# Twelve scatters ahead of a branch, and weight conversions on VectorE begun at the second step, in an attention, mixture-of-experts and MLP kernel

## The chip, the cores and the metric

The kernel runs on one core of one Trainium2 chip. The metric is the device time of one execution in microseconds (us). TensorE is PE in the profile, its weight loads are PEld, VectorE is DVE, ScalarE is ACT, GpSimd is POOL and SyncE, which issues most transfers, is SP.

## The reference

```
attn = attention of q, k, v (2 x 8 heads x 768 x 64), only between tokens whose 6 sign bits agree
x    = attn as 1536 rows of 512
logits = x @ w_gate + log1p(exp(x @ w_noise)) * noise          # 8 experts
top 2 experts of a row, their softmax as weights
out[row] += weight * (relu(x[row] @ w1[e]) @ w2[e])            # e = 0..7, 512 -> 1024 -> 512
h = out @ w_in;  g = h - tanh(h);  result = g @ w_out          # 512 -> 2048 -> 512, weights given as float64
```

## The kernel before

The program has three stages. Attention comes first, then the experts, then the last pair of products. Products are done in split form: an operand is a rounded high part and a low rest, and three matmuls make one product, so each weight tile is copied to `wt` by ScalarE (line 1004) and its low part is made by a subtraction on VectorE or GpSimd (line 1003).

The expert stage works through nine segments in a loop over `n`. Segments 0 and 1 are the two parts of expert 0, and segment `n` from 2 on is expert `n - 1`. A segment has eight steps `f`, one for each 128 columns of the hidden layer. A step does the first product of step `f + 1` (`both_step`, line 1269, and 1276 for a tail), lets ScalarE and VectorE move its result out of PSUM (lines 1300 and 1302), and then does the second product of step `f` (`y_step`, lines 1309 to 1311). Two PSUM banks take turns for the first product. After the last step `y_out` copies the four result banks out (lines 1334 to 1341), and the next segment's tail matmuls wait for the last of these copies.

Behind the products each step has a body, in this order: at its `f` a load of the next segment's rows (`load_x`, lines 1209 and 1212), weight fetches, `store`, transposes of the next segment's rows (`trans_x`, lines 1222 to 1224), conversion steps (`convert_more`), the fetch of the next 64-bit weights (`fetch64`), and one weight tile more (`next_w`). Everything on all five engines is issued in the order in which the program text has it (a manual schedule), so each engine works its instructions off in that order.

The rows of a segment are brought together by scattering. The late batch's gate (`gate(B - 1)`) finds each row's place among the experts' rows, `pick` turns it into indices `sidx`, and `scatter` sends twelve indirect DMAs of 128 rows from GpSimd to `Xg` in DRAM. Segment 1's rows come another way (`gather_x`, two indirect DMAs at line 832), the segments from 2 on are loaded from `Xg`. Between the place and the scatters the gate also makes the experts' counts (`totals`, `excess`), from which the engines take branches. One of them is `overflow`, an arm for rows that don't fit, which isn't taken here.

The last stage's weights arrive as 64-bit floats. `fetch64` loads 1 MB into one of two buffers `cv_t`, and `convert` turns it into float32 in six steps: line 1073 with ScalarE's 1071 in front of it, 1075, 1077, 1079, 1082 and the add at 1084. There are 16 such tiles, 96 steps. `convert_more(n)` takes `n` steps.

Of the kernel before, what the change touches and what calls it, by code (L numbers as in the profile page):

```python
# [6 lines left out]
F32 = mybir.dt.float32  # L7
# [8 lines left out]
ALU = mybir.AluOpType  # L16
# [33 lines left out]

POOL1 = 7

CV1 = 3

CVN = 2

KEEP = 8

ADD = (3, 4, 5, 6)

FA = 4

# [28 lines left out]
def body(tc, q, k, v, proj, w_gate, w_noise, noise, w1, w2, w_in, w_out, out):  # L91
    nc = tc.nc
    PS = bass.MemoryType.PSUM
    B, H, S, D = q.shape
# [22 lines left out]
    with ExitStack() as ctx:  # L117
# [66 lines left out]
        start = ExitStack()  # L184
# [106 lines left out]
        hd = {}  # L291
# [376 lines left out]
        def gate(b):  # L668
            w = lambda name, shape, dt=F32: gx.tile(shape, dt, name=name)
            early = b < B - 1  # L670
# [9 lines left out]
            u = w("g_u", [128, NC, E])  # L680
# [108 lines left out]
            if early:  # L789
# [2 lines left out]
                eng.tensor_scalar(capv[:, 1, 0:1], late0, -1.0, float(CAP), op0=ALU.mult, op1=ALU.add)  # L792
                eng.tensor_copy(basev[:, 1, 0:1], late0)
                eng.tensor_scalar(late0, late0, float(1 - FIRST), None, op0=ALU.add)
            yield
            if not early:
                yield from totals()
                yield from excess()
            ts = w("g_ts", [128, NC, E])
            if early:  # L800
                eng.tensor_scalar(ts, over, BIG, None, op0=ALU.mult)
# [3 lines left out]
            gd[b] = (oh, over, t, v8, e12)  # L805
            for _ in pick(sidx[:, :, b], oh, ts, eng, lead):
                yield

        def hot(b, c):

# [102 lines left out]
        def totals():  # L913
            tot = bank("a")
            for b in range(B):
                for c in range(NC):
                    nc.tensor.matmul(tot[:, b * E:(b + 1) * E], onesb, M[:, b, c], start=(b == 0 and c == 0),
                                     stop=(c == NC - 1), skip_group_check=True)
            for c in range(BC):
                nc.tensor.matmul(tot[:, B * E:(B + 1) * E], onesb, M[:, 1, c], start=False, stop=(c == BC - 1), skip_group_check=True)  # L920
            nc.vector.tensor_copy(tots, tot[:, 0:(B + 1) * E].rearrange("p (b e) -> p b e", b=B + 1))
            yield
            nc.vector.tensor_tensor(cnt, tots[0:1, 0], tots[0:1, 1], op=ALU.add)
            nc.vector.tensor_tensor(cnt[:, 0:1], cnt[:, 0:1], basev[0:1, 1, 0:1], op=ALU.add)
            pick_arms(0, 0, 1)

        def excess():
            nc.vector.tensor_tensor(exs, tots[:, 0], tots[:, 1], op=ALU.add)
            nc.vector.tensor_tensor(exs, exs, capv[:, 1], op=ALU.subtract)
            nc.vector.tensor_scalar(exs, exs, 0.0, None, op0=ALU.max)  # L930
            yield
            cmx = gx.tile([128, 1], F32, name="cmx")
            nc.vector.tensor_reduce(cmx, exs, op=ALU.max, axis=AX.X)
            nc.vector.tensor_copy(cmi, cmx)
            yield
            pick_arms(1, 1, E)
            yield
# [127 lines left out]
        def convert(f, t):  # L1065

            two = lambda dt: t.rearrange("p t n -> p (t n)").bitcast(dt).rearrange("p (n two) -> p n two", two=2)
            hi = two(I32)[:, :, 1]
            tl = lambda name, dt: hd["cvp"].tile([128, 2 * DM], dt, name=name)
            g, p, a, w = tl("cv_g", F32), tl("cv_p", I32), tl("cv_a", I32), tl("cv_w", F32)  # L1070
            nc.scalar.activation(g, two(F32)[:, :, 1], AF.Abs)

            nc.vector.tensor_scalar(g, g, _f32(896 << 20), None, op0=ALU.max)
            yield
            nc.vector.tensor_scalar(p, g.bitcast(I32), 3, 0x3FFFFFF8, op0=ALU.logical_shift_left, op1=ALU.bitwise_and)
            yield
            nc.vector.scalar_tensor_tensor(a, hi, _i32(0xC0000000), p, op0=ALU.bitwise_and, op1=ALU.bitwise_or)
            yield
            nc.vector.tensor_scalar(p, a, _i32(0xFF800000), None, op0=ALU.bitwise_and)
            yield  # L1080
            u = p.bitcast(F32)
            nc.vector.scalar_tensor_tensor(u, two(U32)[:, :, 0], 2.0 ** -52, u, op0=ALU.mult, op1=ALU.mult)  # L1082
            yield
            (nc.gpsimd if hd["n"] in ADD else nc.vector).tensor_tensor(w, u, a.bitcast(F32), op=ALU.add)  # L1084
            stores.append(lambda: nc.sync.dma_start(out=W2f[f], in_=w))
            yield

        def convert_more(n):

            for _ in range(n):  # L1090
                if hd.get("cv") is None and RAW64:
                    hd["cv"] = convert(*RAW64.pop(0))
                if hd.get("cv") is not None and next(hd["cv"], 1) is not None:
                    hd["cv"] = None
                    if RAW64:
                        hd["cv"] = convert(*RAW64.pop(0))
                        next(hd["cv"])
# [16 lines left out]
        def run(f, *a_):  # L1114
            for _ in f(*a_) or ():
                pass
# [118 lines left out]
        def load_arm(n):  # L1235
            e, b = segs[n][:2]
            AV[n] = nc.tensor.value_load(arm[0:1, e:e + 1], min_val=0, max_val=3)
# [225 lines left out]
            fn_()  # L1463
        fill(left[0], KEEP)
        load_arm(1)
        run(scatter, B - 1, 0)
        run(scatter, B - 1, 1)
        start.close()

        mid, late = ExitStack(), ExitStack()  # L1470

# [168 lines left out]
        def put_out():  # L1640
# [11 lines left out]
        manual = lambda: sched.enter_context(tc.manual_schedule(engines={nc.tensor.engine, nc.vector.engine, nc.scalar.engine,  # L1652
                                                                         nc.gpsimd.engine, nc.sync.engine}))
        overflow()
        manual()
        while fn[0] < wn[0] + 4:
            fetch()
# [18 lines left out]
        for n in range(1, NSG):  # L1676
            last = n == NSG - 1
            if last:
                store()
                mid.close()  # L1680
                del rings["st"]
                rings["C2"] = ctx.enter_context(tc.tile_pool(name="wC2", bufs=WC2, reuse_waits="tile"))
                rings["C"] = ctx.enter_context(tc.tile_pool(name="wC", bufs=WC, side="right", reuse_waits="tile"))
                rings["st"] = late.enter_context(tc.tile_pool(name="stC", bufs=2, side="right", reuse_waits="tile"))
            fx = 0 if n <= B else 1
            if n == B:
                free_gate()
            for f in seg_steps(n, (lambda: h2_step(at(0), None)) if last else (lambda: both_step(n + 1, 0))):
                if not last and f == fx:
                    load_x(n + 1)  # L1690
                if last and f == 4:
                    del rings["st"]
                    held_n = fn[0] - 1
                while fn[0] < min(wn[0] + (PF if "st" in rings or n < B else 2), len(wsrc)):
                    fetch()
                store()
                if not last and f == FA:
                    load_arm(n + 1)
                for dc in range(0 if last else KD4):
                    if f == (5 + dc // 2 if n == B - 1 else 3 + dc):  # L1700
                        trans_x(n + 1, dc)
                if n < B:
                    rests(2)
                    assert f < NF - 1 or not rest
                if n > B:
                    next(sort, None)
                if (B, CV1) <= (n, f) < (NSG - 1, 0):
                    hd["n"] = n
                    convert_more(CVN + (n in ADD and f % 4 == 1))
                if (B, 0) <= (n, f) < (NSG - 1, 0):  # L1710
                    while conv64 and len(RAW64) + (hd.get("cv") is not None) < (1 if (n, f) < (B, CV1) else 2):
                        fetch64(conv64.pop(0))
                for j in range(BC if last else 0):
                    if f == j:
                        gather(j)
                    if f == MIX[j]:
                        mix(j)
                        flush(1)
                for j in range(BC if last else 0):
                    if f == JOIN[j]:  # L1720
                        combine(j)
                        flush(1)
                if n >= B or f >= W1:
                    next_w()
                if B <= n < B + WN0 - NF and f == 4 or last and f in TWO:
                    next_w()
                if last and f == 6:
                    assert not [m for m in RAW if m <= held_n]
                    late.close()
                    m2 = ctx.enter_context(tc.tile_pool(name="m2", bufs=2, side="right", reuse_waits="tile"))  # L1730
                    gb2 = m2.tile([128, 1], F32, name="gb2")
                    nc.vector.memset(gb2, G2 / (2 * G3))
                    gsb = m2.tile([128, 1], F32, name="gsb")
                    nc.vector.memset(gsb, -GS)
# [7 lines left out]
        for n in range(-LA, len(steps2)):  # L1742
# [4 lines left out]
            blk, f = at(n + LA) or (NBK, 0)  # L1747
# [47 lines left out]
```

## Time and the profile before

| | |
|---|---|
| median of 3 runs | 888.33 us (886.56 to 890.89) |
| the profiled execution | 892.47 us |
| its span in the trace | 890.7 us |
| TensorE busy | 866.2 us, 97% of the span |
| VectorE, ScalarE, GpSimd busy | 655.6, 536.6, 437.0 us |

The span runs from the first to the last instruction that the profiler recorded. The profiled execution took 1.8 us more than its span, and 4.1 us more than the median of the runs without a profile. All instants below are microseconds from the start of the span.

### The profile page before, as it was taken

How to read it: one execution, taken by the hardware profiler on the slowest of the kernel's cores; microseconds unless marked ns; L12 is line 12 of the kernel's file. 1: busy time of each engine (PE TensorE's matmuls, PEld its weight loads, DVE VectorE, ACT ScalarE, POOL GpSimd, SP SyncE). 2: the span in 40 equal slices, each digit the busy share in tenths (PEclk: the TensorE clock that was granted, in tenths of full speed). 3: DMA queues.
4: the chain of work that ended last, by engine and by line, in shares of the span. 5: the costliest groups of instructions: out<-in, count | busy, mean ns of one | idle time of the engine just before them, and what ended most of it. 6: DMA issues, size and time to landing. Idle time of an engine off the chain costs nothing. (4 is left out here: it accounts for less than half of the span.)

```text
span 890.7 us, 13686 instructions
## 1 busy us (share of the span) xinstructions
PE 866.2 (97%) x4622; PEld 677.3 (76%) x4622; DVE 655.6 (74%) x1261; ACT 536.6 (60%) x1027; POOL 437.0 (49%) x403
## 2 busy tenths in 40 slices
PE   8999999999989979999999999999999999999998
PEld 3556555555546869898879898888889999999996
DVE  7688778778745644888697879867987677677665
ACT  6677668767435234544434445456787677677765
POOL 6787787798876354025312217720432632632322
PEclk9999999999989999999999999999999999999999
DMA  5546645511242467896799697784300200210000
GB/s 125 134 128 198 206 136 167 162 25 40 81 148 84 130 224 240 267 321 195 249 297 316 213 322 234 241 298 137 95 24 1 84 24 1 72 36 1 25 13 36
DMA packets 111980, 127.52 MB, mean 143 GB/s; under 512 B 33744, under 2 KB 82944, under 8 KB 111888
## 3 DMA queue, kind: packets, MB, share of 16 engines
q1 hardware_dynamic: 106880, 110.81, 39.6%
q0 software_dynamic: 5008, 15.49, 5.2%
q8 instruction: 57, 0.93, 0.4%
q14 instruction: 35, 0.29, 0.1%
HBM read 82.81 MB, written 41.18 MB: 139 GB/s over the span
## 5 line engine op out<-in xcount | busy, mean ns | idle before, releaser
L1309 PE MATMUL bank<-wt,hh 128*128 128x512 f32 (+1 forms) x392 | 156.2, 399 | 2.4 <-PEq L1247 1.2
L1588 POOL TENSOR_TENSOR g_th<-g_h,g_th 128x384 f32<-128x384 f32 x64 | 67.1, 1049 | 181.6 <-ACT g_th L1587 181.0
L1311 PE MATMUL bank<-wt,hh 128*128 128x512 f32 (+1 forms) x392 | 155.4, 396 | 0.4 <-DVE hh L1302 0.3
L1310 PE MATMUL bank<-wt,hh 128*128 128x512 f32 (+1 forms) x392 | 154.3, 394 | 0.0
L1269 PE MATMUL bank<-xh,wt 128*128 128x400 f32 (+3 forms) x512 | 140.2, 338 | 0.0
L443 DVE TENSOR_REDUCE mx<-bank 128x1 f32<-128x384 f32 x192 | 103.2, 551 | 42.9 <-PE bank L442 34.3
L478 ACT ACTIVATE p<-bank 128x384 f32<-128x384 f32 x192 | 91.9, 489 | 69.3 <-PE bank L477 56.9
L1269 PEld LDWEIGHTS bank<-xh,wt 128*128 128x128 f32 x512 | 93.7, 191 | 1.4
L1004 ACT ACTIVATE wt<-wraw 128x1024 fp32r<-128x1024 f32 x75 | 78.8, 1055 | 21.4 <-PE bank L1311 17.9
L1084 POOL TENSOR_TENSOR cv_w<-cv_p,cv_a 128x1024 f32<-128x1024 f32 x12 | 33.5, 2792 | 114.7 <-DVE cv_p L1082 46.3
L1311 PEld LDWEIGHTS bank<-wt,hh 128*128 128x128 f32 (+1 forms) x392 | 73.4, 187 | 19.4 <-DVE hh L1613 1.8
L1309 PEld LDWEIGHTS bank<-wt,hh 128*128 128x128 f32 (+1 forms) x392 | 73.8, 188 | 17.5 <-issue 2.7
L1231 PE MATMUL bank<-xh,wt 128*128 128x384 f32 x256 | 86.2, 337 | 0.0
L1229 PE MATMUL bank<-xh,wt 128*128 128x384 f32 x256 | 86.1, 336 | 0.0
L511 POOL TENSOR_TENSOR ps<-ps,p 128x768 f32<-128x768 f32 x45 | 82.4, 1830 | 7.4 <-ACT p L478 2.9
L1230 PE MATMUL bank<-xl,wt 128*128 128x384 f32 x256 | 85.9, 336 | 0.0
L1269 PE MATMUL bank<-xl,wt 128*128 128x400 f32 (+3 forms) x256 | 85.3, 333 | 0.3 <-DVE xl L1224 0.3
L502 PE MATMUL bank<-p,v 128*64 128x384 f32 x384 | 84.5, 519 | 0.9 <-issue 0.9
L1300 ACT ACTIVATE hh<-bank 128x448 fp32r<-128x448 f32 (+2 forms) x72 | 36.2, 503 | 79.0 <-issue 25.4
L1310 PEld LDWEIGHTS bank<-wt,hh 128*128 128x128 f32 (+1 forms) x392 | 73.6, 188 | 13.2
L476 PE MATMUL bank<-qc,kb 108*128 108x384 f32 (+1 forms) x192 | 79.3, 413 | 2.7 <-issue 1.6
L1003 DVE TENSOR_TENSOR wt<-wraw,wt 128x1024 fp32r<-128x1024 f32 (+1 forms) x64 | 75.3, 1182 | 5.2 <-ACT wt L1004 4.9
(318 smaller groups left out, 1864.2 us busy)
## 6 DMA issues: line engine op xcount, KB each, us to landing
wraw<-in_moe_w_dram SPq DMA_DIRECT2D x118, 256.0 KB
cv_t<-in_moe_w_in_dram SPq DMA_DIRECT2D x16, 512.0 KB
cv_t<-in_moe_w_out_dram SPq DMA_DIRECT2D x16, 512.0 KB
W2f<-cv_w SPq DMA_DIRECT2D x16, 512.0 KB
wraw<-W2f SPq DMA_DIRECT2D x16, 512.0 KB
Xg<-zero SPq DMA_DIRECT2D x14, 512.0 KB
xy<-Xg SPq DMA_DIRECT2D x7, 768.0 KB
Y<-xy SPq DMA_DIRECT2D x7, 768.0 KB
```

Of the source, the lines that this page charges most:

```text
L443: nc.vector.tensor_reduce(MX[i % 2][:, c, hf:hf + 1], ps[:, :HF], op=ALU.max, axis=AX.X)
L476: nc.tensor.matmul(ps[:, :HF], KB[sn(g, par)][r, ck(kc)], QC[sn(g, par)][r, half(hf)], start=True, stop=False)
L478: nc.scalar.activation(hd["p", i, kc][:, half(hf)], ps[:, :HF], AF.Exp, scale=float(D) ** -0.5)
L502: nc.tensor.matmul(hd["o", i][hf * D:(hf + 1) * D, :HF], raw["v", g][:, par, kc], hd["p", i, kc][:, half(hf)], start=(kc == 0), stop=(kc = ...
L511: eng.tensor_tensor(t, hd["p", i, 0] if kc == 1 else t, hd["p", i, kc], op=ALU.add)
L1229: nc.tensor.matmul(ps[:, :n], ws(0, dc), xh[:, dc, :n], start=(dc == 0), stop=False)
L1230: nc.tensor.matmul(ps[:, :n], ws(0, dc), xl[:, dc, :n], start=False, stop=False)
L1231: nc.tensor.matmul(ps[:, :n], ws(1, dc), xh[:, dc, :n], start=False, stop=(dc == KD4 - 1))
L1269: nc.tensor.matmul(col(ps), t[:, w_, 0, ck(dc)], col(x_[l_][:, dc]), start=(dc == 0 and (w_, l_) == (0, 0)), stop=(dc == KD4 - 1 and w_ == 1))
L1309: nc.tensor.matmul(ps[:m], a, t[:, 0, 1], start=first, stop=False)
L1310: nc.tensor.matmul(ps[:m], a, t[:, 1, 1], start=False, stop=False)
L1311: nc.tensor.matmul(ps[:m], l, t[:, 0, 1], start=False, stop=last)
```

## The change

Three things are changed in the program text. First, in the late batch's gate `pick` now comes directly behind the places, and `totals` and `excess` follow it; one `yield` of that gate is gone. Second, the manual schedule of the first stage is closed before the late batch's scatters, and a schedule of its own for GpSimd holds over them and over `overflow`, so that GpSimd's twelve scatters come in front of its branch in the order of the text. Third, all adds of the conversion are VectorE's (before, those of segments 3 to 6 were GpSimd's); the conversion begins at step 1 of segment 2 and not at step 3, which also moves the second `fetch64` two steps ahead; and the third conversion step in some steps stands in segment 2 at `f` = 1, 4 and 7, where before it stood in segments 3 to 6 at `f` = 1 and 5.

```diff
-CV1 = 3
+CV1 = 1
 CVN = 2
-ADD = (3, 4, 5, 6)
@@ gate
-            yield
-            if not early:
-                yield from totals()
-                yield from excess()
+            if early:
+                yield
             ts = w("g_ts", [128, NC, E])
@@ gate
             for _ in pick(sidx[:, :, b], oh, ts, eng, lead):
                 yield
+            if not early:
+                yield from totals()
+                yield from excess()
@@ convert
-            (nc.gpsimd if hd["n"] in ADD else nc.vector).tensor_tensor(w, u, a.bitcast(F32), op=ALU.add)
+            nc.vector.tensor_tensor(w, u, a.bitcast(F32), op=ALU.add)
@@ body
         load_arm(1)
+        start.close()
+        order_p = ExitStack()
+        order_p.enter_context(tc.manual_schedule(engines={nc.gpsimd.engine}))
         run(scatter, B - 1, 0)
         run(scatter, B - 1, 1)
-        start.close()
@@ body
         overflow()
+        order_p.close()
         manual()
@@ the loop over segments
                 if (B, CV1) <= (n, f) < (NSG - 1, 0):
-                    hd["n"] = n
-                    convert_more(CVN + (n in ADD and f % 4 == 1))
+                    convert_more(CVN + (n == B and f % 3 == 1))
                 if (B, 0) <= (n, f) < (NSG - 1, 0):
                     while conv64 and len(RAW64) + (hd.get("cv") is not None) < (1 if (n, f) < (B, CV1) else 2):
                         fetch64(conv64.pop(0))
```

## Rows read from the trace of the kernel before

**Rows 1.** Who TensorE waited for, whole span: us in total, times, longest.
```profile
PE bank L1222 <- DMA xy<-Xg: 6.3, 1, 6.3
PE bank L1276 <- DVE xy L1341: 2.4, 3, 2.0
...
PE bank L1276 <- DVE hh L1302: 0.6, 1, 0.6
```

**Rows 2.** TensorE's timeline: start, us, what [idle before it <- releaser].
```profile
332.69 1.98 PE L1222 MATMUL bank<-ident,xy 128*128 128x128 f32 x8 [6.26 <-DMA xy<-Xg]
...
357.42 0.40 PE L1309 MATMUL bank<-wt,hh 128*128 128x512 f32 x1
```

**Rows 3.** Stretches: engines' busy us (instructions), then the granted TensorE clock, DMA share, GB/s.
```profile
332.69:337.06 4.37, 4.37 (x21) 4.19 (x22) 1.25 (x2) 2.03 (x3) 0.78 (x1) 0.50 1.11 344
...
463.36:466.82 3.46, 3.46 (x8) 2.73 (x9) 3.43 (x6) 0.55 (x1) 0.00 (x0) 0.51 1.06 392
```

**Rows 4.** GpSimd's timeline, 297 to 327 us.
```profile
297.91 0.96 POOL L832 DMA_INDIRECT xy<-Xd,xidx  x1 [0.30 <-issue]
302.27 1.77 POOL L851 DMA_INDIRECT Xg<-x,sidx  x1 [3.40 <-DVE sidx L847]
...
314.40 0.98 POOL L851 DMA_INDIRECT Xg<-x,sidx  x1 [6.49 <-DMA Xg<-x,sidx]
...
325.29 0.98 POOL L851 DMA_INDIRECT Xg<-x,sidx  x1 [0.30 <-issue]
```

**Rows 5.** Instructions of the overflow branch: ns min/median/max, first and last start.
```profile
L1474 POOLq EVENT_SEMAPHORE  x4: 17/43/3947, 304.7 to 309.1; - x4
```

**Rows 6.** VectorE's timeline, 296 to 302 us.
```profile
296.33 0.20 DVE L788 TENSOR_TENSOR T<-bank,basev 128x48 f32<-128x48 f32 x1
...
301.01 0.19 DVE L804 SCALAR_TENSOR_TENSOR g_ts<-g_ov,T 128x48 f32<-128x48 f32 x1
...
301.81 0.17 DVE L847 CAST sidx<-g_p 128x12 int32<-128x12 f32 x1
```

**Rows 7.** Timeline of SyncE's queue, 328 to 358 us.
```profile
328.10 0.34 SPq L1209 DMA_DIRECT2D xy<-Xg  x1
...
349.61 0.53 SPq L1062 DMA_DIRECT2D cv_t<-in_moe_w_out_dram  x1
...
357.43 0.70 SPq L1062 DMA_DIRECT2D cv_t<-in_moe_w_out_dram  x1
```

**Rows 8.** Who SyncE's queue waited for, 345 to 361 us.
```profile
SPq L1062 <- DMA cv_t<-in_moe_w_out_dram: 0.3, 1, 0.3
```

**Rows 9.** ScalarE's timeline, 349 to 362 us.
```profile
349.42 0.54 ACT L1300 ACTIVATE hh<-bank 128x448 fp32r<-128x448 f32 x1 [2.91 <-issue]
349.86 1.05 ACT L1004 ACTIVATE wt<-wraw 128x1024 fp32r<-128x1024 f32 x1
...
360.58 1.14 ACT L1071 ACTIVATE cv_g<-cv_t 128x1024 f32<-128x1024 f32 x1
```

**Rows 10.** Timeline of VectorE, 361 to 364 us.
```profile
361.75 0.69 DVE L1073 TENSOR_SCALAR cv_g<-cv_g 128x1024 f32<-128x1024 f32 x1 [0.41 <-ACT cv_g L1071]
...
363.09 1.22 DVE L1003 TENSOR_TENSOR wt<-wraw,wt 128x1024 fp32r<-128x1024 f32 x1
```

**Rows 11.** Instructions on the tile `cv_p`: ns min/median/max, first and last start.
```profile
L1075 DVE TENSOR_SCALAR cv_p<-cv_g x16: 683/694/1672, 362.5 to 566.4; 128x1024 int32<-128x1024 int32 x16
L1077 DVE SCALAR_TENSOR_TENSOR cv_a<-cv_t,cv_p x16: 1206/1224/1716, 365.8 to 569.8; 128x1024 int32<-128x1024 int32 x16
...
L1084 POOL TENSOR_TENSOR cv_w<-cv_p,cv_a x12: 2393/2685/3328, 385.6 to 535.5; 128x1024 f32<-128x1024 f32 x12
L1084 DVE TENSOR_TENSOR cv_w<-cv_p,cv_a x4: 1225/2196/2207, 372.4 to 575.7; 128x1024 f32<-128x1024 f32 x4
```

**Rows 12.** Timelines of GpSimd and VectorE at 456 us.
```profile
455.94 2.40 POOL L1084 TENSOR_TENSOR cv_w<-cv_p,cv_a 128x1024 f32<-128x1024 f32 x1 [14.89 <-DMA W2f<-cv_w]
...
456.14 2.75 DVE L1073 TENSOR_SCALAR cv_g<-cv_g 128x1024 f32<-128x1024 f32 x1 [0.40 <-ACT cv_g L1071]
```

## The prediction, made before the result was known

> **What bounds the kernel now.** I read TensorE's waits first. TensorE works through almost the whole span, so only its few holes and its low clock can be won. The largest is one wait of 6.3 us for the rows `xy` of segment 2; next come waits at the ends of segments for VectorE's last copy, 2.4 us in three pieces, and one of 0.6 us [rows 1]. The timeline puts the large one at 326.43 to 332.69 [rows 2]. [...] The first hole thus costs 6.26 + 2.2 = 8.5 us, the ends of segments 2.4 + 0.6 + 1.6 = 4.6 us.
>
> Then I followed the first hole back. SyncE issued the load at 328.10 [rows 7], 1.8 us after GpSimd was through with the last of twelve scatters (325.29 + 0.98 = 326.27), and it landed 4.6 us later [rows 2]. GpSimd began the train at 302.27, 0.3 us behind its indices, and stood still for 6.49 us after the fourth scatter until earlier scatters had landed [rows 4]. That stop is the branch's: its semaphore waits on GpSimd begin at 304.7 to 309.1, and one lasts 3.95 us [rows 5]. The indices were there at 301.98, although the places `T` were done at 296.53; the four instructions from `ts` to `sidx` take 0.97 us [rows 6].
>
> **Indices earlier, scatters ahead of the branch.** The indices are now ready at 296.53 + 0.97 = 297.5. GpSimd is held by the second `gather_x` until 297.91 + 0.96 = 298.87 [rows 4], so the train starts at about 299.2. Its twelve scatters took 326.27 - 302.27 = 24.0 us with the stop and 17.8 without it, so it ends at 317.0, lands 1.8 us later at 318.8, and the load lands at 323.4. TensorE wants it at 326.43: the hole and its low clock go, -8.5 us. GpSimd's branch now waits for twelve landings, but GpSimd would be free from about 320, and before it was free from 326.3; nothing is late there. The branch's long wait is GpSimd's own [rows 5], and I count none for the other engines.
>
> Two things are paid. `totals` now stands directly behind `find` on TensorE, with no fill between, and takes the PSUM bank that VectorE reads until 296.53: some 0.5 us of idle TensorE, bounded by nothing and 1 us. And the train meets weight fetches in the DMA queues. The first four scatters, issued among such fetches, were done at 307.91 and landed only just before 314.1, some 6 us later and not 1.8 [rows 4]. If all lag like that, the load lands at 327.6 and a hole of 0.7 us stays. I take the free lag, since the fetches that were beside the four are over by the train's end, and keep 0.7 us for the range. Sum of this part: -8.0 us, range -9 to -6.
>
> **Conversion two steps sooner.** This is the edit that I expect to cost. `fetch64` of the first tile stays in step 0 of segment 2, since the body still loads `xy` and one weight tile first. Its second half was issued at 349.61 [rows 7], and its landing shows in the second tile's issue: that one ended a wait for the first at 357.43 [rows 7, 8]. So the tile is there at 357.4, 7.8 us after its issue, behind the load of `xy` (1 MB) and a weight tile (0.5 MB). Before, ScalarE wanted it at 360.58, 3.2 us later, which hid it [rows 9]. Now the conversion's first instruction (L1071) stands in step 1, right behind the eviction that ends at 349.96 [rows 9]. ScalarE works in order: it stands for 7.4 us, and behind it are the next weight copy (1.05 us) and the eviction of step 3's first product (0.54); VectorE's conversion steps wait too, and its L1302 behind them.
>
> TensorE goes on with what it has: the first product of step 3, the second of step 2, and the first of step 4, since the two PSUM banks suffice that far. At 357.42 it comes to the second product of step 3 [rows 2], which needs that eviction. ScalarE: 357.4 + 1.14 + 1.05 + 0.54 = 360.15. VectorE from 358.58: L1073 0.69, L1075 0.69, L1077 1.22, L1003 1.22, L1302 0.55, together 4.4 with no pauses, so 363.0 [rows 10, 11], with L1302 taken as long as ScalarE's eviction. The third matmul of that product, which would run at 357.89, needs VectorE's part: a delay of 363.1 - 357.9 = 5.2 us. Such idle time brought the low clock before [rows 3]; I add 2.0 us, between 1.6 and 2.2. Sum +7.2 us. From below: if the tile landed 2 us earlier and the clock held, +3. From above: the three conversion steps per body at `f` = 4 and 7 leave VectorE late twice more, +9.
>
> **All adds on VectorE.** Twelve adds leave GpSimd (median 2.69 us) and cost VectorE 1.23 us each where nothing disturbs it [rows 11]: 14.8 us over four segments. Segments 3 to 6 lose two steps each, so a segment there does 2.67 tiles of 5.7 us (15.3) instead of three without the add (13.5). That lies beside TensorE's work, except at the end of a segment, where what stands in step 6 delays the copies. Before, it was L1073 and L1075 (1.4 us); now, by counting steps, it is that pair in segment 2, then 1.9 us (add and L1073, L1079 and L1082, or L1075 and L1077). At ends with no spare time that is 0.5 us more each, four or five times: +2.4 us. In return GpSimd's adds no longer hold VectorE: at 456.14 L1073 took 2.75 us instead of 0.69 beside an add, just ahead of the 2.0 us wait [rows 1, 10, 12]. The waits of 2.4 + 0.6 us and the 1.6 us of clock go, -4.6. Net -2.2 us; with no relief it is +2.4, with no new delay -4.6. [...]
>
> **Sum.** -8.0 + 7.2 - 2.2 = -3.0 us on a profiled execution of 892.47 (span 890.7). I take it off the median, 888.33, which lies 4.1 us lower: 885.3 us. About 0.5% (4.4 us) is what a measurement of this kernel can tell from no change.
>
> **Rivals.**
> - *The first tile is there in time, or TensorE's lead covers it.* Then +7.2 becomes about 0: 878.1. For it: the fetch is only 1 MB, and SyncE is no longer blocked before it. Against it: its place in the queue is the same, behind the same load. Chance 0.23.
> - *The train stays choked by fetches.* If eight of the twelve go at the first four's rate, (314.1 - 302.27)/4 = 3.0 us each, and the others at 1.3, the train ends near 328 and the hole stays at about its old size: the first part is worth 0, net +5.0, 893. If only half of that comes about, 889. For it: the lag of the first four; against it: those fetches are a fixed amount. Chance 0.13.
> - [...] Chance 0.10.
> - *The change doesn't do what it says*: scatters or load are held by something else, and the 6.26 us stay while the rest comes: 893. Against it: nothing else of that stretch ends so late. Chance 0.06.
>
> **How the numbers follow.** My forecast has 0.48, with its own range from 882 to 889: 0.14 of it lies below -4.4 us, 0.32 within, 0.02 above. Faster by over 0.5%: 0.14 + 0.23 = 0.37. Slower by over 0.5%: 0.02 + 0.06 of the choked train + 0.10 + 0.04 = 0.22. Within: 0.41. The range, from 877 to 892, takes in the first rival and half of the choked train.
>
> **What would show it.** The last scatter starts by 318, the load is issued by 321, and no wait for `xy<-Xg` is left on TensorE. ScalarE's first L1071 comes directly behind the second eviction of segment 2 with some 7 us of idle time that ended with `cv_t`, and TensorE has a wait of 3 to 6 us two steps later with the clock at 0.5 behind it. L1084 is on VectorE alone at 1.2 us outside segment 7, and L1073 is nowhere over 1.2 us in segments 3 to 6. Most of all the prediction fails if that first tile's wait is absent or covered, or if the loss at the ends of segments doesn't shrink.

## The result, and the profile after

The changed kernel took 902.28 us (median of four executions, 899.49 to 902.95) where the kernel before took 888.73 us (886.56 to 890.89): a ratio of 1.0147, 95% interval 1.0114 to 1.0179. It was 13.6 us slower; 3.0 us faster had been predicted. Four later sessions, each on a chip of its own, measured the same kernel at 884 to 887 us, so the number above can only be understood together with the repeats below. (A session is one sitting on one chip, in which a kernel and the kernel before are timed beside each other.)

The changed kernel's lines are shifted: the branch is L1475, the evictions L1299 and L1301, the second product L1308 to L1310, the scatters L850, the load L1208, the conversion's ScalarE step L1070 and its add L1083. Who TensorE waited for (us in total, times, longest), in the execution of 902.42 us:

```profile
PE bank L1308 <- PEq L1475: 14.2, 1, 14.2
PE bank L1308 <- ACT hh L1299: 2.3, 1, 2.3
PE bank L1310 <- DVE hh L1301: 2.3, 2, 2.0
PE bank L474 <- issue: 1.6, 1, 1.6
...
PE bank L500 <- issue: 0.9, 1, 0.9
...
PE bank L1268 <- DVE xl L1223: 1.0, 1, 1.0
...
PE bank L916 <- DVE T L786: 0.5, 1, 0.5
```

The 6.3 us hole for `xy` and the waits for the last copy and for `hh` at the ends of segments [rows 1] are gone. New are the foreseen waits behind the 64-bit tile (ACT `hh`, DVE `hh`), the foreseen 0.5 us at `totals`, 1.0 us at L1268 (0.3 before), and one large wait that nothing had foreseen: 14.2 us at TensorE's own overflow branch. All four executions of record look alike: their mean granted clock was 0.984 to 0.987, against 0.988 to 0.996 in the 38 later executions of the same kernel. Timelines of TensorE, ScalarE and GpSimd:

```profile
299.69 0.27 PE L1369 MATMUL bank<-xh,wt 128*128 128x192 f32 x1
...
302.39 0.27 PE L1369 MATMUL bank<-xh,wt 128*128 128x192 f32 x1
316.91 0.71 PE L1308 MATMUL bank<-wt,hh 128*96 128x512 f32 x1 [14.24 <-PEq L1475]
...
295.78 0.33 ACT L1299 ACTIVATE hh<-bank 128x192 fp32r<-128x192 f32 x1 [2.72 <-PE bank L1369]
303.86 0.33 ACT L1299 ACTIVATE hh<-bank 128x192 fp32r<-128x192 f32 x1 [7.75 <-PE bank L1369]
316.79 0.33 ACT L1299 ACTIVATE hh<-bank 128x192 fp32r<-128x192 f32 x1 [12.60 <-remote]
364.87 1.12 ACT L1070 ACTIVATE cv_g<-cv_t 128x1024 f32<-128x1024 f32 x1 [7.36 <-DMA cv_t<-in_moe_w_out_dram]
...
299.22 1.03 POOL L850 DMA_INDIRECT Xg<-x,sidx  x1 [0.30 <-DVE exs L927]
...
313.98 0.98 POOL L850 DMA_INDIRECT Xg<-x,sidx  x1 [0.30 <-issue]
```

Read the three engines together. TensorE's last matmul in front of the branch starts at 302.39; the next one runs at 316.91. Beside this GpSimd sends its twelve scatters in one train, 299.22 to 314.96, as planned [rows 4]. ScalarE's rows tell more than TensorE's: the eviction at 303.86 needs a group of matmuls whose last one, at 299.69, ended by the trace at 299.96, and the one at 316.79 (its row says only `remote`) needs the group of 302.39. The first therefore started 3.9 us and the second 14.1 us after the end that the trace gives for its matmuls. TensorE's own semaphore wait at the branch stands at 316.8, beside the second of these evictions (in e5 below it stands at 298.9), and TensorE went on only then. Whether the signals were late or the matmuls themselves, the trace can't tell. Windows (engines' busy us, then granted clock, DMA share, GB/s):

```profile
302.67:316.91 14.24, 0.00 (x1) 0.03 (x1) 3.20 (x7) 0.45 (x2) 9.55 (x10) 0.63 0.80 280
316.91:321.23 4.32, 4.32 (x20) 3.48 (x21) 0.36 (x1) 0.22 (x1) 0.00 (x0) 0.65 0.56 191
```

Behind the hole the clock stood at 0.65 for 4.32 us, 1.5 us of lost work. The predicted 885.3, the hole of 14.2 and this 1.5 make 901.0, near the 902.3 measured; what else the sum leaves out is worked out from the spans further down.

### The profile page after: what moved, and what is told of

Its sections match the earlier page's. It is cut to its first block, busy times and chain, and to the rows that moved or that the text cites. A ratio compares the mean times of both kernels' runs of the same rounds, so it can differ in the third digit from the quotient of the medians.

```text
span 900.6 us, 13682 instructions
## 1 busy us (share of the span) xinstructions
PE 865.4 (96%) x4622; PEld 677.0 (75%) x4622; DVE 665.4 (74%) x1273; ACT 536.1 (60%) x1027; POOL 398.2 (44%) x391
## 5 line engine op out<-in xcount | busy, mean ns | idle before, releaser
L1308 PE MATMUL bank<-wt,hh 128*128 128x512 f32 (+1 forms) x392 | 156.9, 400 | 19.1 <-PEq L1475 14.2
L1310 PE MATMUL bank<-wt,hh 128*128 128x512 f32 (+1 forms) x392 | 156.3, 399 | 2.4 <-DVE hh L1301 2.3
L1268 PE MATMUL bank<-xh,wt 128*128 128x400 f32 (+3 forms) x512 | 139.1, 336 | 0.0
L1002 POOL TENSOR_TENSOR wt<-wraw,wt 128x512 fp32r<-128x512 f32 x30 | 44.9, 1518 | 156.3 <-DMA W2f<-cv_w 146.6
L1308 PEld LDWEIGHTS bank<-wt,hh 128*128 128x128 f32 (+1 forms) x392 | 73.7, 188 | 34.6 <-issue 16.9
L1268 PEld LDWEIGHTS bank<-xh,wt 128*128 128x128 f32 x512 | 92.8, 189 | 1.4
L1310 PEld LDWEIGHTS bank<-wt,hh 128*128 128x128 f32 (+1 forms) x392 | 73.7, 188 | 22.2 <-DVE hh L1301 3.4
L1299 ACT ACTIVATE hh<-bank 128x448 fp32r<-128x448 f32 (+2 forms) x72 | 36.1, 502 | 83.6 <-PE bank L1275 19.4
L1268 PE MATMUL bank<-xl,wt 128*128 128x400 f32 (+3 forms) x256 | 84.8, 331 | 1.0 <-DVE xl L1223 1.0
```

The costliest lines, as they stand in the source:

```text
L1002: low = lambda eng, h: eng.tensor_tensor(t[:, 1, h], r[:, h], t[:, 0, h].bitcast(F32), op=ALU.subtract)
L1268: nc.tensor.matmul(col(ps), t[:, w_, 0, ck(dc)], col(x_[l_][:, dc]), start=(dc == 0 and (w_, l_) == (0, 0)), stop=(dc == KD4 - 1 and w_ == 1))
L1308: nc.tensor.matmul(ps[:m], a, t[:, 0, 1], start=first, stop=False)
L1310: nc.tensor.matmul(ps[:m], l, t[:, 0, 1], start=False, stop=last)
```

## The experiments

**The two parts, each alone.** The theory (A) was that TensorE's code or signals behind its branch wait for GpSimd's train. The first two runs undo one part each:

```diff
 e1: changed kernel, conversion as before
-CV1 = 1
+CV1 = 3
+ADD = (3, 4, 5, 6)
-            nc.vector.tensor_tensor(w, u, a.bitcast(F32), op=ALU.add)
+            (nc.gpsimd if hd["n"] in ADD else nc.vector).tensor_tensor(w, u, a.bitcast(F32), op=ALU.add)
-                    convert_more(CVN + (n == B and f % 3 == 1))
+                    hd["n"] = n
+                    convert_more(CVN + (n in ADD and f % 4 == 1))
 e2: kernel before with these lines the other way round
```

> The scatter part of the change alone: indices in front of the counts, twelve scatters ahead of GpSimd's branch; the conversion as before. Theory A (TensorE's code behind its own overflow branch comes only when GpSimd's train is through, and the conversion part is worth about +1.5 us): a TensorE hole of about 14 us at the branch, no hole for xy, some 897 us. Rival C (the hole comes from the conversion part or from both together): no hole at the branch, some 880 us.

> The conversion part alone: begun two steps sooner, all adds on VectorE; gate and scatters as before. Theory A: no hole at the branch, the 6.3 us hole for xy is back, ScalarE stands some 7 us for the first 64-bit tile, TensorE loses about 4 us behind it and a clock step, the ends of segments win 4.6 us: 889 to 891 us. Rival C: 14 us hole at the branch here too, 902 us or more.

The scatter part alone took 880.84 us, ratio 0.9922 (0.9899 to 0.9946); the conversion part alone 892.54, ratio 1.0043 (1.0025 to 1.0062). The instructions of the first are those of the changed kernel up to the branch and well past it, its twelve scatters stand ahead of the branch as well, and its TensorE has no hole there. As a rule of this program theory A fell with that, and so did its number (897). That session holds no run of the unedited changed kernel, though, so e1 can't say what that one would have done there. The second lies 1.5 us above what was expected; in its trace the hole for `xy` is back with 5.9 us, and there is no hole at the branch. The two ratios together give 0.9965, some 885 us.

**How many scatters ahead of the branch.** The diff is that of e3, with four ahead; in e4 (none) and e8 (eight) the 4 is a 0 and an 8.

```diff
-        run(scatter, B - 1, 0)
-        run(scatter, B - 1, 1)
+        train = [st for wh in range(2) for st in [scatter(B - 1, wh)] * NC]
+        for st in train[:4]:
+            next(st)
...
         overflow()
+        for st in train[4:]:
+            next(st)
         order_p.close()
```

> The changed kernel with four scatters ahead of GpSimd's branch and eight behind it. Theory A (the hole ends when the scatters that stand ahead of the branch are through): the hole at TensorE's branch ends near 306 us (about 3.6 us long instead of 14.2), and the train ends near 323, so that 0 to 4 us of hole for xy come back: 888 to 894 us. Rival D (the hole is the branch's meeting with any scatter train, its size does not go by the number ahead of it): 14 us hole, some 902 us.

> The changed kernel with all twelve scatters behind GpSimd's branch, the indices still early. Theory A: no hole over 1.5 us at TensorE's branch, the train starts near 302 and ends near 319, no hole for xy: 902.3 - 14.2 - 2 (clock) = 886 us. Rival E (the hole comes from the new order on TensorE, with the totals directly behind the places, and not from the scatters): 14 us hole stays, some 902 us.

> The changed kernel with eight scatters ahead of GpSimd's branch and four behind it. By theory G as with none or four ahead: 885 to 887 us, no hole over 1.5 us at the branch. If the hole needs a long train ahead of the branch: a hole of about 9 us, some 896 us.

886.78 us, ratio 0.9982 (0.9960 to 1.0003), with four; 886.0, 0.9973 (0.9951 to 0.9995), with none; 888.29, 1.0008 (0.9986 to 1.0030), with eight. No hole at the branch in any; TensorE waited 1.1 us for `xy` with four, 1.4 with eight, and not at all with none. The intervals overlap each other and that of the unedited kernel below (0.9972 to 1.0006); eight ahead came out 1.3 us over what was expected. The order of scatters and branch is thus worth nothing that can be measured once the indices are early. In e4 the train ended only at 316.90, 5.7 us later than in e5 below, but its load went out only 1.4 us behind e5's (timeline of SyncE's queue in e4):

```profile
318.97 0.34 SPq L1208 DMA_DIRECT2D xy<-Xg  x1
```

Late indices with all twelve ahead were not run, so what the order would be worth alone isn't shown.

**The changed kernel again, and with one half of the conversion part undone.** The other two edits of this set:

```diff
 e6: adds of segments 3 to 6 on GpSimd again (as in e1), CV1 = 1
 e7: adds on VectorE
-CV1 = 1
+CV1 = 3
-                    convert_more(CVN + (n == B and f % 3 == 1))
+                    convert_more(CVN + (n in (3, 4, 5, 6) and f % 4 == 1))
```

> The changed kernel once more, nothing edited, beside the three others. The scatter part alone ran without a hole at the branch, with the same instructions up to it. Theory F (the hole is fixed by the program as built, later code included): 14 us hole again, some 902 us. Theory G (the hole is a state of the execution or of the chip it ran on, which the scatter train makes possible): no hole here, 885 to 887 us, the sum of the two parts alone (880.8 + 4.3).

> The changed kernel with the adds of segments 3 to 6 on GpSimd again. Without the hole at the branch, as by theory G: 885 to 889 us (the ends of segments lose about 3 us again, VectorE's steps get shorter). By theory F the hole may be there or not; with it 900 to 904 us.

> The changed kernel with the conversion begun at step 3 of segment 2 as before, and the third step of a body where it stood before; adds on VectorE alone. Without a hole at the branch: the wait for the first 64-bit tile is gone, 878 to 881 us (880.8 for the scatter part alone, 0 to 3 us less for the adds). By theory F with the hole: 893 to 897 us.

The unedited changed kernel now took 886.51 us (ten executions, 883.49 to 889.23), ratio 0.9989 (0.9972 to 1.0006). Its waits, timelines (TensorE, ScalarE, GpSimd, SyncE) and one window:

```profile
PE bank L1308 <- ACT hh L1299: 3.5, 1, 3.5
PE bank L1310 <- DVE hh L1301: 2.4, 2, 2.1
...
PE bank L1268 <- DVE xl L1223: 1.0, 1, 1.0
```

```profile
298.63 0.27 PE L1369 MATMUL bank<-xh,wt 128*128 128x192 f32 x1
299.05 0.45 PE L1308 MATMUL bank<-wt,hh 128*96 128x512 f32 x1
...
349.70 0.50 PE L1308 MATMUL bank<-wt,hh 128*128 128x512 f32 x1 [3.50 <-ACT hh L1299]
...
352.64 0.79 PE L1310 MATMUL bank<-wt,hh 128*128 128x512 f32 x1 [2.08 <-DVE hh L1301]
...
298.94 0.33 ACT L1299 ACTIVATE hh<-bank 128x192 fp32r<-128x192 f32 x1 [2.37 <-PE bank L1369]
347.15 1.12 ACT L1070 ACTIVATE cv_g<-cv_t 128x1024 f32<-128x1024 f32 x1 [8.57 <-DMA PT<-tab,posi]
...
295.46 1.03 POOL L850 DMA_INDIRECT Xg<-x,sidx  x1 [0.30 <-DVE exs L929]
...
310.22 0.98 POOL L850 DMA_INDIRECT Xg<-x,sidx  x1 [0.31 <-issue]
...
317.52 0.33 SPq L1208 DMA_DIRECT2D xy<-Xg  x1
```

```profile
349.70:354.00 4.30, 2.22 (x5) 1.45 (x6) 4.23 (x7) 1.33 (x2) 0.97 (x1) 0.55 0.45 140
354.00:358.00 4.00, 4.00 (x17) 3.42 (x16) 2.85 (x5) 1.12 (x2) 0.89 (x2) 0.63 0.58 113
```

The group that ended near 298.9 is evicted at 298.94, and TensorE is through its branch at 299.05, in the middle of the same train. What is left are the waits behind the 64-bit tile: ScalarE stands 8.57 us in front of L1070 (the releaser named there is another transfer; in the first session's trace it is the tile, with 7.36 us).

With the adds undone (e6) it took 888.41 us, ratio 1.0004 (0.9980 to 1.0028); with the conversion begun at step 3 again and the third steps back in their places (e7) 877.85 us (four executions, 877.00 to 879.05), ratio 0.9885 (0.9864 to 0.9907). The latter beats both kernels. TensorE's waits in the expert stage, first of the scatter part alone (e1: L1277 and L1303 are the copies and the eviction at a segment's end), then of e7:

```profile
PE bank L1277 <- DVE xy L1342: 2.7, 3, 1.5
...
PE bank L1277 <- DVE hh L1303: 1.2, 1, 1.2
```

```profile
PE bank L1268 <- DVE xl L1223: 0.3, 1, 0.3
PE bank L1310 <- DVE hh L1301: 0.3, 1, 0.3
...
PE bank L1275 <- DVE xy L1340: 0.2, 1, 0.2
```

**Does the hole come back?** In three more sessions the unedited kernel (e9, e12, e13) ran beside one edit each: every scatter issued twice (e10), 2048 pieces of 128 bytes copied beside the train (e11), or four scatters ahead (e14).

```diff
 e10
-        run(scatter, B - 1, 0)
-        run(scatter, B - 1, 1)
+        for _ in range(2):
+            run(scatter, B - 1, 0)
+            run(scatter, B - 1, 1)
 e11
         load_arm(1)
+        small = dram.tile([4 * DM, 32], F32, name="small")
+        nc.scalar.dma_start(out=small.rearrange("(e k) n -> e k n", e=4), in_=w1[0:4, :, 0:32])
```

> The changed kernel a third time, nothing edited, in another session. Ten executions of it ran near 886.5 us with no hole at the branch, four of the first session near 902 us. Theory G1 (the hole belongs to a chip or session and comes back on some): 899 to 903 us with a hole of some 14 us at the branch if this is such a one. Theory G2 (the hole belonged to the first session alone): 884 to 889 us, and the prediction's sum holds.

> The changed kernel with every one of the twelve scatters issued twice, 24 in a row ahead of GpSimd's branch (the second time the same rows go to the same places). If a long train in itself is what can hold TensorE's code or its signals back (theory A in a weaker form, with a threshold above twelve): a hole of over 5 us at TensorE's branch, beside the later load. If trains do not do that here: no hole over 1.5 us at the branch; the train ends near 326 instead of 311, the load is issued near 333 and lands near 338, so that the hole for xy is 14 to 18 us, and the time some 903 us.

> The changed kernel with one more transfer, issued by ScalarE directly in front of its overflow branch: 2048 pieces of 128 bytes from DRAM to DRAM, beside the scatter train. Theory H (traffic beside the train is what delays the signals of TensorE's matmuls): signals of the matmul groups in front of the branch come late by 1 us or more, a hole of 2 to 15 us at TensorE's branch, 888 to 902 us. If such traffic does not do it: no hole over 1.5 us at the branch, 884 to 890 us.

> The changed kernel a fourth time, nothing edited, in another session. Theory G1 (the hole belongs to a chip or session and comes back on some): 899 to 903 us with a hole of some 14 us at the branch if this is such a one. Theory G2 (the first session alone): 883 to 889 us, no hole at the branch.

> The changed kernel a fifth time, nothing edited, in another session. Theory G1 (the hole belongs to a chip or session and comes back on some): 899 to 903 us, a hole of some 14 us at the branch, and 3 to 4 us lost near 250 us from the start, as in the two profiles of the first session. Theory G2 (the first session alone): 883 to 889 us.

> Four scatters ahead of the branch, beside the run before it in the same session. If that one has the hole: theory A (its length goes by the scatters ahead) gives 3 to 5 us of hole and 888 to 893 us here, theory D (any train) 14 us and 902 us. If that one has none: 884 to 889 us.

The unedited kernel took 884.28, 885.21 and 884.71 us: ratios 0.9971 (0.9951 to 0.9992), 0.9970 (0.9953 to 0.9988) and 0.9976 (0.9958 to 0.9995). None of its three profiles has a wait at the branch. Four ahead: 885.93 us, ratio 0.9988 (0.9964 to 1.0011), again with 1.1 us for `xy`. With the small pieces it took 884.34 us, ratio 0.9969 (0.9952 to 0.9987), without a hole, though in the stretch from 290 to 320 us their queue's 2064 packets took 5.6% of the DMA engines' time. The doubled train took 902.86 us, ratio 1.0173 (1.0137 to 1.0209). The time was as expected for a train without a hole at the branch, but the place was not; VectorE's and TensorE's timelines:

```profile
316.85 0.25 DVE L845 TENSOR_REDUCE g_p<-g_t 128x12 f32<-128x96 f32 x1
331.88 0.17 DVE L846 CAST yidx<-g_p 128x12 int32<-128x12 f32 x1 [14.78 <-DMA Xg<-x,sidx]
...
335.98 0.79 PE L1310 MATMUL bank<-wt,hh 128*128 128x512 f32 x1 [15.01 <-DVE hh L1301]
```

VectorE came to `yidx` at 317.1 and stood there for 14.78 us until scatters to `Xg` released it, with the eviction (L1301) that TensorE needed behind it. In e5, with twelve scatters, the same instruction started at 317.15, with scatters to `Xg` named as releaser too, just behind the end of GpSimd's branch: four semaphore waits there, the longest 3.33 us and ended at 316.2, and then an `INC_SWDGE_SEM` up to 317.0. The branch's rows on GpSimd in e5:

```profile
L1475 POOLq EVENT_SEMAPHORE  x4: 17/43/3332, 309.6 to 312.9; - x4
...
L1475 POOLq INC_SWDGE_SEM  x1: 704/704/704, 316.3 to 316.3; - x1
```

**What the first session's two profiles have in common.** Waits of the kernel before, and a window behind them in three traces (before, changed in the first session, changed in e5):

```profile
PE bank L476 <- issue: 1.6, 1, 1.6
...
PE bank L502 <- issue: 0.9, 1, 0.9
```

```profile
249.98:258.43 8.45, 7.34 (x23) 2.91 (x23) 4.28 (x10) 2.73 (x6) 7.05 (x8) 0.61 0.75 262
```

```profile
250.16:258.50 8.34, 7.23 (x23) 2.92 (x23) 4.24 (x10) 2.72 (x6) 6.91 (x8) 0.59 0.73 258
```

```profile
248.37:256.00 7.63, 7.63 (x45) 4.16 (x43) 4.99 (x14) 3.67 (x8) 6.57 (x8) 1.00 0.94 310
```

Up to some 253 us the first batch's twelve scatters go out (from 237, in before as in e5). In both profiles of the first session TensorE stood still beside them for 1.6 and 0.9 us with no releaser that the trace shows, and ran at 0.61 and 0.59 of its clock behind it. In no later trace is there such a wait; in e5 the clock there is 1.00 (the later traces have 2.2 us at L516 instead, near 265 us). By TensorE's next matmuls in step with each other (L1369, 301.19 there and 297.42 in e5) this had cost 3.8 us in all. That is near the 4.1 us by which the profiled execution of before lay over its median, but whether the executions beside it went without this loss is not on record.

The first session's traces also lack records. Of all semaphore updates they hold 9902 (before) and 9807 (changed), and every later trace at least 10314. What is missing lies beside the trains: up to 230 us the counts agree (3302 and 3301, 3301 in e5), from 230 to 260 they are 241 and 236 against 442, from 260 to 290 they agree again, and from 290 to 330 they are 411 and 255, against 556 in e2 (with the scatters of before) and 699 in e5. TensorE's own updates are 904 in the changed kernel's trace and 909 in e5.

## Why the prediction was right or wrong

**The step that failed** is "The branch's long wait is GpSimd's own [rows 5], and I count none for the other engines." In the session of record TensorE stood 14.2 us at that branch, a wait that the prediction had put at nothing. Taking the spans, 900.6 and 882.9 us, the 17.7 us between the first session and e5 are 3.8 us near 250 us and 14.1 us at the branch (316.91 - 299.05 = 17.86 in all). What follows cancels out: 1.5 us of clock behind the hole, against waits behind the 64-bit tile that are 1.3 us shorter (2.29 + 1.98 for 3.50 + 2.08).

**What caused it is not settled.** The program as built isn't enough: it ran without the hole in four sessions (four traces, and by their times all 38 executions). Nor did a number of scatters ahead of the branch (none, four, eight, twelve), a train of 24, or small transfers beside it bring the hole about. But these edits ran only in sessions in which the unedited kernel has no hole, or wasn't run; what they would have done in the first session is open, and so is whether the chip, the session or the recording made the difference. That it has to do with the trains is likely, as both places and the missing records lie beside one, but it was only seen, not brought about.

The end that the trace gives for a matmul and the start of what needs its result lay 3.9 and 14.1 us apart here, so a full row of matmuls isn't proof that they had finished. The missing updates of the first session show that its recording was incomplete beside the trains, and not that it held TensorE back; no run here shows that it was the cause.

**Scatter part, -8.0 predicted (-9 to -6).** e1 measured -0.78%, -6.9 us (-9.0 to -4.8). The hole for `xy` went, the 0.5 us at `totals` came. The 2.2 us that the sum has for the clock behind the hole are 0.50 of 4.37 us [rows 3]; no run measured that term by itself, and e1, without the hole, ran at a mean clock of 1.00. The working was off where it didn't cost: the train took 15.7 us (e5: 295.46 to 311.20) and not 17.8, but the load was issued only 6.3 us behind it, at 317.52. The lag that I had read from the first four scatters (some 6 us) and then set aside held for all twelve: the longest semaphore wait of GpSimd's branch ended at 316.2, 5.0 us behind the train, and the branch's `INC_SWDGE_SEM` at 317.0. With none ahead (e4) the load went out 2.1 us behind the train, which fits that the order is worth so little. It was still in time: 0 to 0.2 us of wait for `xy` in the four later profiles.

**Conversion sooner, +7.2 predicted (+3 to +9).** e7 against e5, in one session: +1.04%, +9.2 us, just over the upper end; e6 against e1, across two sessions: +0.82%, +7.3 us. The mechanism was the predicted one, term by term in e5: TensorE waited 3.50 + 2.08 = 5.6 us (5.2 predicted); the clock stood at 0.55 and 0.63 for 8.3 us, a loss of 0.45 x 4.3 + 0.37 x 4.0 = 3.4 us, of which 0.9 lie in the idle 2.08 us: 2.5 us of work (2.0 predicted); and a wait at L1268 grew from 0.3 to 1.0 us, which I hadn't counted. Together that is 8.8 us.

**Adds on VectorE, -2.2 predicted.** e5 against e6: -0.15%, -1.3 us; e7 against e1, across two sessions: -0.37%, -3.3 us. The intervals overlap in both pairs, so the size isn't settled; the waits are clearer. The waits for VectorE at the ends of segments, 2.7 + 1.2 us in e1, shrank to 0.2 in e7, and the +2.4 that I had set against it didn't come: the backlog of 0.5 us at a segment's end was no delay. VectorE's busy time rose by 8.7 us from e1 to e7 (655.2 to 663.9) where twelve adds at 1.22 are 14.7, so 6.0 us came back from its other instructions. Of the 4.6 us of relief in the sum 1.6 were clock: rows 3 give 0.49 x 3.46 = 1.7 us behind a wait of 2.0, but in e1, whose waits at the ends of segments are 1.5 us at most, the mean clock was 1.00, so e7 had no such loss to win back from it.

**Sum, -3.0 predicted, 885.3 us.** Without the hole four sessions gave -0.11% to -0.30%, -1.0 to -2.7 us, and 884.3 to 886.5 us: within the range, and by the mechanisms predicted. That the sum comes out so near is luck in part: the scatter part won about 1 us less than predicted, the conversion cost up to 2 us more, and a difference of 1 to 3 us is near what the intervals resolve. The number of record, 902.3, is the same program with 14.1 us at the branch and 3.8 us near 250 us. Of the rivals none was this one: that of the choked train came nearest in place, but saw only the load's lateness, and never asked what else stands still beside a train.

## What to carry to other kernels

Look up indices early: here that was worth 0.8% (e1, with the twelve scatters ahead), and with early indices the order of scatters and branch nothing that could be measured. Before a consumer is moved ahead, ask when its transfer lands and not when it is issued; two steps sooner cost 7 to 9 us here, and with the old start the same kernel is the fastest version of this study (877.85 us). A result that has a new hole with no cause in the program is measured again in another session before it is explained: the first explanation here, complete with times, did not hold in a second session.

## What the runs showed of the hardware

- In one session, ScalarE's evictions started 3.9 and 14.1 us after the end that the trace gives for TensorE's matmuls, beside a train of scatters, with TensorE standing and its granted clock at a mean of 0.63 meanwhile; in e5 both evictions followed after 0.04 us, and in the traces of three more sessions (e9, e12, e13) TensorE has no wait at that branch. In that session nearly half of the semaphore updates beside the first train are missing from both traces (241 and 236 for the 442 of e5).
- Scatters in such a train mostly started every 1.29 us (e5), and with all twelve ahead of GpSimd's branch the load that needs them went 6.3 us behind the train in e5, of which 5.0 were GpSimd's last long semaphore wait. With none ahead it went 2.1 us behind it (e4).
- In e10 VectorE stood 14.78 us in front of `yidx` until scatters released it, rows that `yidx` doesn't use, and TensorE stood 15.01 us for the eviction behind it.
